# A gated mix of infini-attention and ReGLU on one core: the first chunk of x in four loads, four q products side by side, and a new written-out order of all engines

## The chip, the cores and the metric

The kernel runs on one core of a Trainium2 chip. The metric is the device time of one execution in microseconds (us); less is better. Five engines have queues of their own: TensorE (PE, whose weight loads are listed apart as PEld), VectorE (DVE), ScalarE (ACT), GpSimd (POOL) and SyncE (SP, which here only starts DMAs). Each engine runs its own list of instructions in order and waits on semaphores for the others.

## The reference

```python
# x: [1, 2048, 512] bf16; 32 heads of 16; 4 segments of 512 tokens; F = 1792
g = sigmoid((x * gate_w).sum(-1, keepdims=True))
# a: attention within a segment, and a memory M, z carried from segment to segment
for s in range(4):
    qs, ks, vs = q[:, :, s], k[:, :, s], v[:, :, s]          # q = x @ wq and so on
    p = softmax(qs @ ks.T * 0.25 + causal_mask)
    a_mem = (phi(qs) @ M) / (phi(qs) @ z + 1e-6)
    o_s = sigmoid(beta) * a_mem + (1 - sigmoid(beta)) * (p @ vs)
    M = M + phi(ks).T @ vs;  z = z + phi(ks).sum()           # phi(t) = t + 1 if t > 0 else exp(t)
a = concat(o_s) @ wo
# b: gated feed-forward
b = (relu(x @ W_gate) * (x @ W_up)) @ W_down
out = g * a + (1 - g) * b                                     # [1, 2048, 512] bf16
```

## The kernel before, in words

`program` (the body of `build_kernel`) writes down some 1,485 operations, each with the engine that may run it, what it reads and writes, and a cost. `Sched.run` then puts them on the engines in an order that is written out by hand: the table `ORDER` lists, for each engine, the numbers of the operations (a number counts the operations as `program` creates them). `Sched` derives the semaphore waits from what each operation reads and writes. Its costs, `LAND0`, `DCOST` and `landing`, are the planner's estimates of when a load lands; they served in the search for the order. `BANKS` gives one of eight PSUM banks to each product group (an `Epoch`). A product can start only when the engine that copies the bank's former content out of PSUM is done.

The work goes by segments of 512 tokens (a chunk of x). For each segment there are the q, k and v projections (`proj`, lines 574 and 576: products of 128x128 by 128x512, four over the features for each result), the attention (`att`), the memory products (`mu`, `nd`), the gate and up products with ReLU (`ffn`, line 800), and the output products (`outp`, lines 830 and 837). All are interleaved over segments by `ORDER`.

In `att` the scores of one segment are made in 18 *quads*. A quad (line 689) is up to 16 small products, four at a time in the four row groups of the array, that fill four PSUM banks with 2048 scores a partition. One ScalarE exponential (line 700) reads all four banks; GpSimd masks the diagonal parts (line 708); `pv` (line 738) multiplies the exponentials with v. There are 72 quads and 16 `pv`.

The start is special. The first chunk of x isn't transposed by a DMA. SyncE loads it as two halves of the tokens (`ldhT0`, `ldhT2`, 256 KB each) into the buffer hT, TensorE transposes it with an identity (line 511: eight operations `xt` of two products each, one for each half h and feature tile kt), and DVE or ACT copies the result into xT (line 518, `xc`). Until x comes, TensorE multiplies ones (line 502: five products of 512 columns and six of 128). The names of the loads: `ldwq0` to `ldwq3` are the four feature tiles of wq (128 KB each), likewise wk and wv; `ldwg0_k`, `ldwu0_k` the first half of the gate and up weights' columns (224 KB each), `ldwg1_k`, `ldwu1_k` the second half, which the operations `wg0_7` and later read; `ldx1_k` the transposing loads of the second chunk; `ldxr` plain loads of 128 rows of x, from which DVE computes the mixing gate (line 537, `gate0` to `gate15`, into the tile gl).

The kernel also warms ScalarE's exponential (`tab`, line 474) and starts three 1 KB loads from ScalarE (`ldtouch`, into adT).

Of the kernel before, what the change touches and what calls it, by code (L numbers as in the profile page):

```python
# [17 lines left out]
DCOST = {"ldwg0_0": 1000.0, "ldbraw": 1800.0, "ldgwb": 1300.0, "ldx1_0": 1500.0, "vsh0": 1100.0, "vsh1": 1100.0, "vsh2": 1100.0, "vsh3": 1100.0}  # L18
LAND0 = {"ldhT0": 2850.0, "ldhT2": 3100.0, "ldwq0": 3150.0, "ldwq1": 3200.0, "ldwq2": 3100.0, "ldwq3": 3000.0}
# [3 lines left out]
SPLIT = {2: (2,), 4: (4,), 5: (4, 1), 6: (4, 2)}  # L23
CORDER = [[(0, 1, 7, 2, 6, 3, 5, 4), (4, 0, 1, 7, 2, 6, 3, 5)] * 2] * 4
BANKS = ("130453107213460547754000000570000447000004700055766574475646577645465476647467556655640576747455500000450000656000104500"
         "045657464754775776575664507457667554544570454745665500000570000567000006700045657677645665465655776754467567546467670577"
         "54726660000067000067000004500045445454545645656647647546563023146")
ORDER = {k: [int(x) for x in v.split()] for k, v in {
    "pe": """
# [16 lines left out]
1459 1446 1440 1465 1460 1441 1447 1442 1466 1461 1448 1462 1449 1450 1467 1451 1468 1452 1469 1470 1471 1475 1472 1476 1477 1478 1479 1480 1481 1482""",  # L46
    "act": """
# [4 lines left out]
1272 129 1278 1052 1290 1296 1302 1189 1391 1308 1338 1314 1409 1326 1332 1415 1433 1453 1463""",  # L52
    "dve": """
# [9 lines left out]
1288 1421 1422 1322 1323 1345 1344 1346 1434 1324 1347 1348 1349 1350 1443 1473 1483""",  # L63
    "pool": """
# [8 lines left out]
1316 1335 1333 1334 1336 1330 1340""",  # L73
    "sp": """
0 1 2 3 7 6 8 9 4 11 15 5 21 17 13 10 12 16 14 26 18 85 37 23 19 83 156 20 22 36 38 24 182 81 25 181 199 200 39 30 27 157 29 45 87 28 42 31 40 43 92
44 94 93 96 98 100 41 468 469 470 347 346 544 107 471 109 543 105 371 111 370 527 492 113 106 532 120 542 694 502 537 888 118 122 512 887 693 718 119
717 124 522 876 126 871 846 886 836 881 1222 131 1205 1210 866 1221 856 132 1215 1220 1180 1170 1190 1444 1200 1454 1464 1474 1484""",
# [825 lines left out]
```

## Time and profile before

| | |
|---|---|
| median of 3 runs | 265.17 us (264.95 to 265.46) |
| profiled execution, its own time | 265.06 us |
| span of the profiled execution | 263.0 us |
| PE busy | 254.9 us (97%) |
| ACT, DVE, POOL busy | 185.6, 176.7, 121.3 us |
| DMA | 19.86 MB, mean 76 GB/s |

The span runs from the first to the last instruction of the profile; 2.06 us of the execution's own time lie outside it. "Idle before, releaser" in a row of the timeline is the time for which that engine had nothing running before the instruction, and what ended it.

### The profile page before, as it was taken

Reading aid. Unit: us, or ns where it says so; the run is one execution under the profiler, and the core shown is the slowest. Engines: PE = TensorE matmul, PEld = TensorE weight load, DVE = VectorE, ACT = ScalarE, POOL = GpSimd, SP = SyncE. Lnnn points to the kernel's source line nnn. Section 1 sums busy time; section 2 is a strip of 40 time slices with the busy share of each in tenths; the row PEclk is TensorE's granted clock in tenths of the full one; section 3 lists DMA queues with packets and bytes.
Section 4 is the critical chain, followed back from the end, with each engine's and each line's share of the span. In section 5 each row is a group of like instructions: output and inputs, shape, how many; then the busy total and the mean of one; then the engine's idle time right before and its main releaser. Section 6 shows DMA issues by size and latency. Waiting matters only on the chain.

```text
span 263.0 us, 6393 instructions
## 1 busy us (share of the span) xinstructions
PE 254.9 (97%) x2617; PEld 113.9 (43%) x2653; DVE 176.7 (67%) x350; ACT 185.6 (71%) x162; POOL 121.3 (46%) x295
## 2 busy tenths in 40 slices
PE   8999989999999999999999999999999999999996
PEld 4334433434444454444453544444444444444444
DVE  2587578878777477877788667677877533585821
ACT  4588777889888888887986667778676775674001
POOL 2024544665656455463846376636238342716000
PEclk9999999999999999999999999999999999999999
DMA  6998974009263221300036303000115101000002
GB/s 201 312 243 196 224 191 45 23 21 294 51 142 83 63 62 43 61 3 2 0 85 135 72 0 82 2 0 2 31 35 124 23 0 42 20 2 2 0 23 79
DMA packets 34924, 19.86 MB, mean 76 GB/s; under 512 B 24016, under 2 KB 34128, under 8 KB 34896
## 3 DMA queue, kind: packets, MB, share of 16 engines
q1 hardware_dynamic: 34800, 19.46, 30.3%
q8 instruction: 21, 0.34, 0.6%
q10 hardware_dynamic: 96, 0.00, 0.2%
q14 instruction: 7, 0.06, 0.1%
HBM read 10.40 MB, written 2.11 MB: 48 GB/s over the span
## 4 chain that ended last, share of the span: by engine, by line
PE 93%; DVE 2%; issue 2%; DMA 2%
PE ps L800 36%; PE ps L837 19%; PE ps L576 10%; PE ps L689 8%; PE ps L738 6%; PE ps L574 5%; PE ps L830 5%; DMA osb<-in_A_x_dram 2%; PE ps L632 1%; PE ps L502 1%; PE ps L511 1%; PE ps L615 0%; DVE osb L537 0%; DVE hT L811 0%; DVE Mc L620 0%
## 5 line engine op out<-in xcount | busy, mean ns | idle before, releaser
L700 ACT ACTIVATE E<-ps 128x2048 bf16<-128x2048 f32 x72 | 135.1, 1876 | 39.1 <-PE ps L689 38.7
L708 POOL TENSOR_SCALAR_AFFINE_SELECT E<-E 64x256 bf16<-64x256 bf16 (+1 forms) x256 | 101.2, 422 | 100.3 <-ACT E L700 89.5
L800 PE MATMUL ps<-xT,wu 128*128 128x512 bf16 x217 | 60.1, 380 | 1.5 <-issue 0.6
L800 PE MATMUL ps<-xT,wg 128*128 128x512 bf16 x214 | 58.2, 379 | 1.3 <-issue 1.0
L837 PE MATMUL ps<-wd,hT 128*128 128x512 bf16 (+2 forms) x227 | 56.4, 366 | 1.2 <-issue 1.0
L811 DVE TENSOR_TENSOR hT<-ps,rl 128x512 bf16<-128x512 f32 x56 | 38.2, 687 | 27.6 <-PE ps L800 25.8
L800 PEld LDWEIGHTS ps<-xT,wg 128*128 128x128 bf16 x224 | 20.8, 98 | 25.8 <-issue 1.9
L837 PEld LDWEIGHTS ps<-wd,hT 128*128 128x128 bf16 x238 | 21.3, 98 | 23.9 <-issue 3.0
L800 PEld LDWEIGHTS ps<-xT,wu 128*128 128x128 bf16 x224 | 19.6, 98 | 26.1 <-issue 4.7
L746 DVE STREAM_TRANSPOSE Tn<-ps 128x512 f32<-128x512 f32 x32 | 21.4, 699 | 10.6 <-PE ps L738 10.6
L689 PE MATMUL ps<-qT,kp 32*128 32x384 bf16 (+7 forms) x512 | 28.6, 287 | 0.0
L809 DVE TENSOR_SCALAR rl<-ps 128x512 bf16<-128x512 f32 x30 | 20.6, 688 | 8.0 <-PE ps L800 7.9
L808 ACT ACTIVATE rl<-ps 128x512 bf16<-128x512 f32 x26 | 15.5, 596 | 9.8 <-PE ps L800 9.8
L755 POOL TENSOR_TENSOR adT<-Tn,rdg 128x512 bf16<-128x512 f32 x12 | 12.9, 1074 | 14.7 <-DVE rdg L753 14.6
L689 PEld LDWEIGHTS ps<-qT,kp 32*128 32x128 bf16 x512 | 8.2, 92 | 24.9 <-issue 13.1
L845 DVE TENSOR_SCALAR osb<-ps,omg 128x512 bf16<-128x512 f32 (+2 forms) x13 | 9.2, 710 | 14.6 <-PE ps L830 8.8
L738 PE MATMUL ps<-E,vaug 64*17 64x128 bf16 (+7 forms) x512 | 18.7, 283 | 0.0
L738 PE MATMUL ps<-E,vsh 64*17 64x128 bf16 (+7 forms) x512 | 18.3, 283 | 0.0
L576 PE MATMUL ps<-xT,wk 128*128 128x512 bf16 x63 | 17.7, 380 | 0.1
L576 PE MATMUL ps<-xT,wq 128*128 128x512 bf16 x60 | 17.4, 380 | 0.4 <-issue 0.3
L574 PE MATMUL ps<-wv,xT 128*128 128x512 bf16 x62 | 16.7, 380 | 0.3 <-issue 0.2
L830 PE MATMUL ps<-wo,oT 128*128 128x512 bf16 (+2 forms) x67 | 16.4, 366 | 0.2 <-issue 0.2
(67 smaller groups left out, 216.1 us busy)
## 6 DMA issues: line engine op xcount, KB each, us to landing
vsh<-vaug SPq DMA_DIRECT2D x8, 272.0 KB, 3.6
osb<-in_A_x_dram SPq DMA_DIRECT2D x16, 128.0 KB, 2.6
out_dram<-osb SPq DMA_DIRECT2D x15, 128.0 KB, 2.0
wg<-in_B_W_gate_dram SPq DMA_DIRECT2D x8, 224.0 KB, 3.9
wu<-in_B_W_up_dram SPq DMA_DIRECT2D x8, 224.0 KB, 3.8
wd<-in_B_W_down_dram SPq DMA_DIRECT2D x1, 1792.0 KB, 7.8
hT<-in_A_x_dram SPq DMA_DIRECT2D x2, 256.0 KB, 3.0
wq<-in_A_wq_dram SPq DMA_DIRECT2D x4, 128.0 KB, 3.4
```

Of the source, the lines that this page charges most:

```text
L574: ins = e.matmul(A(ep)[:, :], lhsT=V.xT[:, kt, tok + col * 128:tok + (col + 1) * 128], rhs=w[:, kt, :], start=(kt == 0), stop=(kt == KT - 1))
L576: ins = e.matmul(A(ep)[:, :], lhsT=w[:, kt, col * 128:(col + 1) * 128], rhs=V.xT[:, kt, tok:tok + 512], start=(kt == 0), stop=(kt == KT - 1))
L689: ins = q.matmul(dst, lhsT=V.kp[r, kslot(s, G), c, :], rhs=V.qT[r, qslot(s, G), q0:q0 + w], start=True, stop=True, tile_position=(32 * jj, ...
L700: return a.activation(V.E[:, base * 512 + c0:base * 512 + c0 + n], PF[:, x.bank * 512:x.bank * 512 + n], ACT.Exp, scale=SCALE)
L708: pool(lambda g, ap=ap, lim=lim, pat=pat: g.affine_select(out=ap, in_=ap, compare_op=ALU.is_ge, fill=0.0, base=lim, pattern=[[0, 4]] + pat ...
L738: ins = q.matmul(A(eps[p])[32 * jj:32 * jj + 17, 64 * (c + u):64 * (c + u + n)], lhsT=v[:, 8 * G + 2 * jj + p, :], rhs=V.E[r, f:f + 64 * n ...
L746: dve(lambda e, p=p, ep=eps[p]: e.transpose(V.Tn[:, 2 * (G % (TNN // 2)) + p, :], A(ep)[:, :]), t_dve(512), writes=[f"Tn{2 * (G % (TNN // ...
L800: ins = e.matmul(A(ep)[:, :], lhsT=w[:, kt, f * 128:(f + 1) * 128], rhs=V.xT[:, kt, c % XR * 512:(c % XR + 1) * 512], start=(kt == 0), sto ...
L809: ("dve", lambda e, ep=eg, r=r: e.tensor_scalar(V.rl[:, r, :], A(ep)[:, :], 0.0, None, ALU.max), t_dve(512))],
L811: dve(lambda e, ep=eu, r=r, hs=hs: e.tensor_tensor(V.hT[:, hs, :], A(ep)[:, :], V.rl[:, r, :], ALU.mult), t_dve(512), reads=[f"rl{r}"], wr ...
L830: ins = e.matmul(A(ep)[:, 0:c1 - c0], lhsT=V.oT[:, ot[G], i * 128:(i + 1) * 128], rhs=V.wo[:, G, c0:c1], start=st_ and G == 0, stop=sp_ an ...
L837: ins = e.matmul(A(ep)[:, 0:c1 - c0], lhsT=V.hT[:, slots[f], i * 128:(i + 1) * 128], rhs=V.wd[:, f, c0:c1], start=st_ and f == f0, stop=sp ...
```

## The change

1. The first chunk of x is loaded in four pieces of 128 KB instead of two of 256 KB: half h of the tokens, half f of the features, in the order (h0, f0), (h1, f0), (h0, f1), (h1, f1). A row's run in memory is 512 bytes a token instead of 2 KB for two tokens.
2. The transposes run in that order too, and the copies are shared out anew: DVE has those of feature tiles 0 and 2, ACT those of 1 and 3. Three 128-column products of ones instead of six stand before them.
3. The q products of the first segment go feature tile by feature tile for all four results in four banks, and only then come the k products. Before, q and k were mixed.
4. The first wq tile is loaded by ScalarE, behind the warming exponential, which is now ScalarE's first instruction. The three 1 KB loads are gone.
5. The planner's landing times are changed (later landings between 5 and 45 us), and the order of all engines and the banks are searched anew. Every operation after the loads has a number lower by one. Ten of the operations that may run on either engine move from DVE to ACT.
6. `att` is rewritten so that a quad could be split over several visits; the table `SEVEN` that would do so is empty, so each of the 72 visits is one whole quad of the same products. The exponential's view of PSUM and E is now three-dimensional.

The loads in the code, with all else cut:

```diff
-LAND0 = {"ldhT0": 2850.0, "ldhT2": 3100.0, "ldwq0": 3150.0, "ldwq1": 3200.0, "ldwq2": 3100.0, "ldwq3": 3000.0}
+LAND0 = {"ldwq0": 2750.0, "ldwq1": 3200.0, "ldwq2": 3100.0, "ldwq3": 3000.0}
...
+SEVEN = [(), (), (), ()]
...
+    act(lambda e: e.activation(V.eb[:, 0:8], nc.const_aps.tensor(1.0, [128, 8], BF16), ACT.Exp), 1450, writes=["eb"], name="tab")
     x0 = A_x[0, 0:512, :].rearrange("(h p i) d -> h p i d", h=2, i=2)
     for h in range(2):
-        load("sp", [f"hT{2 * h}", f"hT{2 * h + 1}"], V.hT[:, 2 * h:2 * h + 2, :], x0[h], 1 << 18)
+        for f in range(2):
+            load("sp", [f"hx{h}_{f}"], V.hT[:, 2 * h:2 * h + 2, 256 * f:256 * f + 256], x0[h, :, :, 256 * f:256 * f + 256], 1 << 17)
     for eng, nm, w, src in (("sp", "wq", V.wq, A_wq), ("sp", "wk", V.wk, A_wk), ("sp", "wv", V.wv, A_wv)):
         for kt in range(KT):
-            load(eng, [f"{nm}{kt}"], w[:, kt, :], src[kt * 128:(kt + 1) * 128, :], 1 << 17)
+            load("act" if (nm, kt) == ("wq", 0) else eng, [f"{nm}{kt}"], w[:, kt, :], src[kt * 128:(kt + 1) * 128, :], 1 << 17)
...
-    act(lambda e: e.activation(V.eb[:, 0:8], nc.const_aps.tensor(1.0, [128, 8], BF16), ACT.Exp), 1450, writes=["eb"], name="tab")
-    for n, w in enumerate((W_g, W_u, W_d)):
-        load("act", [f"touch{n}"], V.adT[0:16, 32 * n:32 * n + 32], w[0:16, 0:32], 1024)
...
-    for m, n, role in ((5, 512, "w"), (6, 128, "w2")):
+    for m, n, role in ((5, 512, "w"), (3, 128, "w2")):
...
-    for h, kt, eng in ((0, 0, "dve"), (0, 1, "act"), (0, 2, "act"), (1, 0, "dve"), (0, 3, "dve"), (1, 1, "act"), (1, 2, "dve"), (1, 3, "act")):
+    for h, kt, eng in ((0, 0, "dve"), (0, 1, "act"), (0, 2, "dve"), (0, 3, "act"), (1, 0, "dve"), (1, 1, "act"), (1, 2, "dve"), (1, 3, "act")):
...
-                    return a.activation(V.E[:, base * 512 + c0:base * 512 + c0 + n], PF[:, x.bank * 512:x.bank * 512 + n], ACT.Exp, scale=SCALE)
+                    return a.activation(V.E[:, n * 512:(n + k) * 512].rearrange("q (b n) -> q b n", n=512)[:, :, 0:W], PS[:, x.bank:x.bank + k, 0:W], ACT.Exp, scale=SCALE)
```

The numbers of `ORDER` with their names put in, where the prediction speaks of them (a name stands once for each of its operations; `q0_2` is result 2 of q in segment 0, one product each time; `k0_2` and `v0_2` two products each time):

```
PE before: warm warm xt0 xt2 xt1 xt4 xt5 xt3 xt7 xt6 q0_3 q0_0 q0_3 q0_1 q0_0 k0_1 k0_0 k0_1 k0_0 k0_2 q0_2 q0_0 k0_2
           q0_0 q0_3 q0_1 q0_1 k0_3 q0_1 q0_3 k0_3 v0_0 quad ...
PE after:  warm warm xt0 xt1 xt4 xt5 xt2 xt3 xt6 xt7 q0_0 q0_1 q0_2 q0_3 (four times) k0_0 k0_3 k0_2 k0_1
           k0_0 k0_1 k0_3 k0_2 v0_2 v0_1 quad ...
PE before, later: pv0_0 mu0 quad wg0_7 q1_1 wg0_7 q1_0 q1_0 q1_1 quad wu0_7 ...
PE after, later:  pv0_0 mu0 quad k1_1 k1_0 k1_1 q1_1 k1_0 q1_1 quad q1_0 wg0_7 q1_0 wg0_7 wg0_8 wg0_8 wg0_10 quad wu0_7 ...
DVE before: ... hm0_6 tr0_0_1 tr0_0_0 gate3 reb mum0 qcp1_0 ...
DVE after:  ... hm0_5 tr0_0_0 reb tr0_0_1 gate3 gate1 kcp1_0 gate4 kmask0_2_1 mum0 ...
SP before: hT0 hT2 wq0 wq1 wk1 wk0 wk2 wk3 wq2 ...     ldxr3 is the 45th, ldwg1_1 the 35th, ldwu1_3 the 48th
SP after:  hx0_0 hx1_0 hx0_1 hx1_1 wq1 wq2 wq3 wk0 wk1 wk2 wk3 wv0 ...     ldxr3 is the 42nd, ldwg1_1 the 45th, ldwu1_3 the 50th
```

(`xt4` to `xt7` are those of the second half of the tokens; `mum0` on DVE empties the bank of `mu0`; `reb` is a reciprocal.)

More of the change, by code (lines that the diff above doesn't have):

```diff
@@ L670, in visit @@
             for G, c, u, n in parts:
-                for jj in range(4):
-                    f = jj * W + o
-                    while f < jj * W + o + 64 * n:
-                        g = min((f // 512 + 1) * 512, jj * W + o + 64 * n)
-                        steps.append((f - jj * W, jj, G, c, 64 * (c + u) + f - jj * W - o, f, g - f))
-                        f = g
+                steps.append((o, G, c, 64 * (c + u), 64 * n))
                 for v in range(n):
-                    at.setdefault((G, c), {})[u + v] = (base * 512, W, o + 64 * v, vid)
+                    at.setdefault((G, c), {})[u + v] = (base * 512, 512, o + 64 * v, vid)
                 if u == 0:
@@ L681, in visit @@
                 o += 64 * n
-            steps.sort(key=lambda x: (x[0], -x[1]))
-            def fq(q):
-                for _, jj, G, c, q0, f, w in steps:
-                    r = slice(32 * jj, 32 * jj + 32)
-                    i, j = part[f // 512]
-                    dst = PS[:, eps[i].bank + j, f % 512:f % 512 + w]
-                    ins = q.matmul(dst, lhsT=V.kp[r, kslot(s, G), c, :], rhs=V.qT[r, qslot(s, G), q0:q0 + w], start=True, stop=True, tile_position=(32 * jj, 0), skip_group_check=True)
-                return ins
@@ L703, in visit @@
-            runs = [[d] for d in diag]
-            for i, xs in enumerate(runs):
-                dims, pat = ([[xs[1] - xs[0], len(xs)]], [[0, len(xs)]]) if len(xs) > 1 else ([], [])
-                for h, lim in ((64, 0), (128, 64)):
-                    ap = bass.AP(V.E[:].tensor, base * 512 + xs[0], [[NBLK * 512, h], [W, 4]] + dims + [[1, 64]])
-                    pool(lambda g, ap=ap, lim=lim, pat=pat: g.affine_select(out=ap, in_=ap, compare_op=ALU.is_ge, fill=0.0, base=lim, pattern=[[0, 4]] + pat + [[1, 64]], channel_multiplier=-1),
-                                      t_pool(256 * len(xs)), reads=[f"E{base + j}" for j in range(nb)] + ([f"V{vid}m0_{i}"] if lim else []), writes=[f"V{vid}m{lim}_{i}"], name=f"mask{name}")
@@ L710, in visit, with fx @@
-            vres[vid] = [f"E{base + j}" for j in range(nb)] + [f"V{vid}m{lim}_{i}" for lim in (0, 64) for i in range(len(runs))]
+            return base, W, vid, steps, diag, sorted({p[0] for p in parts})
+        def visit(pieces):
+            eps, todo, rd = [], [], set()
+            for (base, W, vid, steps, diag, Gs), rows in pieces:
+                ep = Epoch("main", len(rows))
+                eps.append(ep)
+                for o, G, c, q0, w in steps:
+                    todo += [(o, -j, ep, i, G, c, q0, w) for i, j in enumerate(rows)]
+                rd |= {f"kp{kslot(s, G)}_{h}" for G in Gs for h in range(2)} | {f"qT{qslot(s, G)}" for G in Gs}
+            for x in eps:
+                x.group = eps
+            todo.sort(key=lambda x: x[:2])
+            def fq(q):
+                for o, j, ep, i, G, c, q0, w in todo:
+                    r = slice(-32 * j, 32 - 32 * j)
+                    ins = q.matmul(PS[:, ep.bank + i, o:o + w], lhsT=V.kp[r, kslot(s, G), c, :], rhs=V.qT[r, qslot(s, G), q0:q0 + w], start=True, stop=True, tile_position=(-32 * j, 0), skip_group_check=True)
+                return ins
+            W = max(x[0][1] for x in pieces)
+            name = f"{s}_{pieces[0][0][5][0]}_{vctr[0]}"
+            vctr[0] += 1
+            pe(fq, W / 2.4 + 10.0, reads=sorted(rd), writes=[x.res for x in eps[1:]], name=f"quad{name}", mode="r", ep=eps[0], role="w")
+            for ((base, W, vid, steps, diag, Gs), rows), x in zip(pieces, eps):
+                k, n = len(rows), base + rows[0]
+                def fx(a, x=x, W=W, k=k, n=n):
+                    return a.activation(V.E[:, n * 512:(n + k) * 512].rearrange("q (b n) -> q b n", n=512)[:, :, 0:W], PS[:, x.bank:x.bank + k, 0:W], ACT.Exp, scale=SCALE)
+                act(fx, t_act(k * W), writes=[f"E{n + i}" for i in range(k)], name=f"exp{name}", ep=x, role="r")
+                left[vid] = left.get(vid, 4) - k
+                if left[vid] == 0:
+                    for i, o in enumerate(diag):
+                        for h, lim in ((64, 0), (128, 64)):
+                            ap = bass.AP(V.E[:].tensor, base * 512 + o, [[NBLK * 512, h], [512, 4], [1, 64]])
+                            pool(lambda g, ap=ap, lim=lim: g.affine_select(out=ap, in_=ap, compare_op=ALU.is_ge, fill=0.0, base=lim, pattern=[[0, 4], [1, 64]], channel_multiplier=-1),
+                                 t_pool(256), reads=[f"E{base + j}" for j in range(4)] + ([f"V{vid}m0_{i}"] if lim else []), writes=[f"V{vid}m{lim}_{i}"], name=f"mask{s}_{Gs[0]}_{vid}")
+                    vres[vid] = [f"E{base + j}" for j in range(4)] + [f"V{vid}m{lim}_{i}" for lim in (0, 64) for i in range(len(diag))]
@@ L754, in flush @@
             av = V.adT[:, :].rearrange("q (c p e) -> q p c e", p=2, e=16)
-            (dve if s == NSEG - 1 else pool)(lambda e: e.tensor_tensor(av, Tv[:, :, :, 0:16], gv.unsqueeze(3).to_broadcast([128, 2, 16, 16]), ALU.mult), 690 if s == NSEG - 1 else 1100, reads=tn + [f"rdg{G % 2}"], writes=["adT"] + ([f"touch{n}" for n in range(3)] if s + G == 0 else []), name=f"ad{s}_{G}")
+            (dve if s == NSEG - 1 else pool)(lambda e: e.tensor_tensor(av, Tv[:, :, :, 0:16], gv.unsqueeze(3).to_broadcast([128, 2, 16, 16]), ALU.mult), 690 if s == NSEG - 1 else 1100, reads=tn + [f"rdg{G % 2}"], writes=["adT"], name=f"ad{s}_{G}")
             os_ = (s * 4 + G) % OTN
@@ L765, in att @@
         last = {G: max(i for i, t in enumerate(todo) if t[0] == G) for G in range(4)}
-        i0 = 0
-        for k, units in enumerate(UNITS[s]):
+        i0, quads, ends = 0, [], {}
+        for units in UNITS[s]:
             parts = []
@@ L773, in att, with get @@
                     parts.append([G, c, u, 1])
+            quads.append((parts, [G for G in range(4) if i0 <= last[G] < i0 + units]))
             i0 += units
-            visit(parts)
-            while carry and carry[0][3] < qctr[0] - 1:
+        made = {}
+        def get(k):
+            if k not in made:
+                made[k] = quad(quads[k][0])
+            return made[k]
+        k, visits = 0, []
+        while k < len(quads):
+            if k in SEVEN[s]:
+                visits += [[(k, A4)], [(k + 1, (0, 1, 2))], [(k + 2, A4)], [(k + 1, (3,)), (k + 3, (0, 1))], [(k + 4, A4)], [(k + 3, (2, 3)), (k + 5, (0,))], [(k + 6, A4)], [(k + 5, (1, 2, 3))]]
+                k += 7
+            else:
+                visits.append([(k, A4)])
+                k += 1
+        for n, v in enumerate(visits):
+            visit([(get(k), rows) for k, rows in v])
+            while carry and all(left.get(x) == 0 for x in carry[0][3]) and carry[0][4] < vctr[0] - 1:
                 flush()
-            if k == 0:
+            if n == 0:
                 between()
                 vsh_dma(s)
-            for G in range(4):
-                if i0 - units <= last[G] < i0:
-                    carry.append((s, G, at, qctr[0] - 1))
+            for k, rows in v:
+                for G in quads[k][1]:
+                    if left[made[k][2]] == 0:
+                        carry.append((s, G, at, [made[j][2] for j in range(len(quads)) if j in made and any(p[0] == G for p in quads[j][0])], vctr[0] - 1))
         if s == NSEG - 1:
```

63 lines of the change are left out of this document (25 added, 38 removed), and 74 rows, old and new, of the table ORDER.

## The prediction

> **What bounds the kernel now.** I read the page's busy times first, then PE's own list of waits, then busy time by stage, then the timeline of the two stages in which PE loses something.
>
> ```profile
> span 263.0 us, 6393 instructions
> PE 254.9 (97%) x2617; PEld 113.9 (43%) x2653; DVE 176.7 (67%) x350; ACT 185.6 (71%) x162; POOL 121.3 (46%) x295
> PEclk9999999999999999999999999999999999999999
> PE 93%; DVE 2%; issue 2%; DMA 2%
> ```
>
> PE is busy for 97% of the span at full granted clock, and the chain that ended last is PE for 93%. So only what PE waits for, or does too early or too late, can change the time. PE's list of waits, longest in total first (total, times, longest):
>
> ```profile
> PE ps L800 <- issue: 1.6, 10, 0.2
> PE ps L837 <- issue: 1.0, 6, 0.2
> PE ps L502 <- PEq L888: 0.8, 1, 0.8
> PE ps L800 <- DVE Mc L620: 0.5, 1, 0.5
> ```
>
> The "issue" waits are many of at most 0.2 us. They stand where PE goes between quads, `pv` and full products. Counted in the two order tables, there are 164 such changes before and 164 after, and no two quads are neighbours in either. So this cost stays. Only one wait on another engine is longer than 0.2 us. By stage (start:end, length, PE busy, PEld, DVE, ACT, POOL, clock, DMA share, GB/s):
>
> ```profile
> 5.30:12.30 7.00, 6.95 (x31) 2.67 (x31) 3.68 (x10) 3.74 (x9) 0.00 (x0) 1.00 0.97 304
> 36.40:37.00 0.60, 0.06 (x1) 0.07 (x2) 0.60 (x3) 0.55 (x1) 0.55 (x2) 1.00 0.48 158
> 37.00:255.00 218.00, 214.14 (x2277) 95.10 (x2309) 153.36 (x302) 159.06 (x134) 109.90 (x260) 1.00 0.21 49
> 255.00:263.00 8.00, 5.66 (x43) 3.34 (x41) 0.97 (x2) 1.27 (x2) 0.00 (x0) 1.00 0.24 78
> ```
>
> From 37 to 255 us PE idles 3.9 of 218 us, in the small steps above: nothing to win there, only to lose. The tail (2.3 us without PE) is the last piece's copy and store; both orders end with seven pairs of 128-column products and an output product, so I cost it at nothing. Two places are left: the head up to 12.3 us, and a hole of 0.54 us at 36.4.
>
> **The head, now.** Timeline (start, length, engine, what; idle before and who ended it):
>
> ```profile
> 0.80 1.28 ACT L518 ACT_TABLE_LOAD   x1 [0.80 <-PEq L888]
> 0.81 0.86 SPq L448 DMA_DIRECT2D hT<-in_A_x_dram  x2
> 0.84 2.93 PE L502 MATMUL ps<-const-bfloat16-1.0 128*128 128x512 bf16 x11 [0.84 <-PEq L888]
> 1.65 0.15 PEld L502 LDWEIGHTS ps<-const-bfloat16-1.0 128*128 128x128 bf16 x1 [0.28 <-issue]
> 1.72 0.90 SPq L448 DMA_DIRECT2D wq<-in_A_wq_dram  x2
> 2.08 0.15 PEld L502 LDWEIGHTS ps<-const-bfloat16-1.0 128*128 128x128 bf16 x1 [0.28 <-issue]
> 3.67 1.67 PE L511 MATMUL ps<-ident,hT 128*128 128x128 bf16 x16
> 4.10 0.42 DVE L518 CAST xT<-ps 128x256 bf16<-128x256 f32 x1 [4.10 <-PE ps L511]
> 4.39 0.77 PEld L511 LDWEIGHTS ps<-ident,hT 128*128 128x128 bf16 x10 [0.17 <-DMA hT<-in_A_x_dram]
> 4.53 1.45 ACT L518 ACTIVATE xT<-ps 128x256 bf16<-128x256 f32 x4 [2.44 <-PE ps L511]
> 5.31 1.25 PE L576 MATMUL ps<-xT,wq 128*128 128x512 bf16 x5
> 5.85 0.22 ACT L474 ACTIVATE eb<-const-bfloat16-1.0 128x8 f32<-128x8 bf16 x1
> 6.53 0.55 PEld L576 LDWEIGHTS ps<-xT,wk 128*128 128x128 bf16 x4 [0.47 <-DMA wk<-in_A_wk_dram]
> 7.53 0.98 PEld L576 LDWEIGHTS ps<-xT,wk 128*128 128x128 bf16 x6 [0.45 <-DMA wk<-in_A_wk_dram]
> 12.39 0.10 PEld L689 LDWEIGHTS ps<-qT,kp 32*128 32x128 bf16 x4 [0.42 <-ACT qT L582]
> ```
>
> The first q product starts at 5.31. The order puts 31 full products between there and the first quad, which starts about 0.1 us after the last of them (12.39), so they end at 12.29. The pace of such products is that of this piece of the chain (start, length, what), 0.216 us each:
>
> ```profile
> 52.03 2.16 PE ps L574 x10
> ```
>
> 31 x 0.216 = 6.70 us, but 12.29 - 5.31 = 6.98: 0.28 us are lost in the head, where the weight loads wait for wk.
>
> **The head, after.** Let S be the start of the first q product; the 31st product then ends at S + 6.70 if no load is late. S is the latest of three things.
>
> (a) *x and its transposes.* The two 256 KB loads let PE go at 3.67 and 4.39, 0.72 us apart, so 128 KB are worth 0.36: the first quarter is there at 3.67 - 0.36 = 3.31. SP starts a load each 0.45 us (0.81 to 1.72 for two), so the others come at 3.76, 4.21, 4.66. Four products each at 0.10 (1.67 us for 16) fit into 0.45, so PE ends the transposes at about 5.1. The first tile of features needs only the quarters of 3.31 and 3.76. DVE's copy starts 0.43 after its product (3.67 to 4.10) and takes 0.42; the second is done at 3.76 + 0.85 = 4.61. The first q result also takes over the bank of a transpose that ACT copies (0.36, a quarter of 1.45): two products later, 4.78.
>
> (b) *wq0.* The table load ends at 2.08, the warming exponential takes 0.22, so ScalarE starts the load at 2.30. This start hides before ACT's first copy (3.9 at the earliest). Landing: the wq loads took (minimum, median, maximum), and a 1 KB load from ScalarE took 2.4:
>
> ```profile
> DMA to landing us min/median/max: 3.0/3.4/3.7
> adT<-in_B_W_gate_dram ACTq DMA_DIRECT2D x1, 1.0 KB, 2.4
> ```
>
> So between 4.7 and 5.7 (2.4 and 3.4); I take 3.0, the value of the first wq load, which also went out while x was on its way: 5.30. It is (b) that decides: S = 5.3, no earlier than before.
>
> (c) *the rest.* Feature tile 1 is needed at S + 0.86 = 6.2; wq1 is now SP's fifth load, out at 2.6, landing at 3.4 later at 6.0. The next tiles have 0.86 each against 0.47 between loads. The k products start at S + 3.45 = 8.8, when wk0 and wk1 (eighth and ninth, out at 4.1 and 4.5) are there since about 8. In the new order the loads that PE waited for come before their use.
>
> So the 31st product ends at 5.3 + 6.70 = 12.0 against 12.29: **-0.3 us**. Ends: S = 5.1 gives -0.5, S = 5.7 gives +0.1. The three ones-products less remove nothing: they'd end at 0.84 + 5 x 0.43 + 3 x 0.10 = 3.3, when x lands. (0.43 is the step from the row at 1.65 to that at 2.08.)
>
> **The hole at 36.4.**
>
> ```profile
> 31.09 0.52 SPq L536 DMA_DIRECT2D osb<-in_A_x_dram  x1
> 32.48 1.31 DVE L746 STREAM_TRANSPOSE Tn<-ps 128x512 f32<-128x512 f32 x2 [0.33 <-PE ps L738]
> 33.53 0.38 PE L800 MATMUL ps<-xT,wg 128*128 128x512 bf16 x1 [0.16 <-issue]
> 35.38 0.93 DVE L537 CUSTOM_DVE_ANT_0 osb<-osb,gwb 128x512 bf16<-128x512 bf16 x1 [1.59 <-DMA osb<-in_A_x_dram]
> 36.51 0.37 DVE L620 TENSOR_TENSOR Mc<-Mc,ps 128x272 f32<-128x272 f32 x1
> 36.94 0.60 PE L800 MATMUL ps<-xT,wu 128*128 128x512 bf16 x2 [0.54 <-DVE Mc L620]
> ```
>
> SP started ldxr3 only at 31.09; it landed 4.3 us later. DVE stood 1.59 us before `gate3`, `mum0` came late, and PE waited 0.54 us for `mu0`'s bank. After, ldxr3 is SP's 42nd load instead of the 45th, some three starts (about 3 us at this stage) earlier, so it lands near 32.4, before DVE is through its transposes (33.8 now). And `mu0`'s bank is next used by `wg0_10`, 14 products later than `wu0_7` was. What is late next on DVE: `gate1` and `gate4` stand before `mum0` too, 0.93 each, which that distance (3 us) covers. So **-0.54 us**; ends -0.6 and 0 (if ldxr1 or ldxr4 are late instead).
>
> **The rest of the order.** The same products, quads and `pv`. Ten copies move from DVE to ACT, 0.6 us each by the profile's groups (mean in ns, then idle before):
>
> ```profile
> L700 ACT ACTIVATE E<-ps 128x2048 bf16<-128x2048 f32 x72 | 135.1, 1876 | 39.1 <-PE ps L689 38.7
> L809 DVE TENSOR_SCALAR rl<-ps 128x512 bf16<-128x512 f32 x30 | 20.6, 688 | 8.0 <-PE ps L800 7.9
> L808 ACT ACTIVATE rl<-ps 128x512 bf16<-128x512 f32 x26 | 15.5, 596 | 9.8 <-PE ps L800 9.8
> ```
>
> ACT goes from 185.6 to 191.6 us of 263: cover enough on average, but quads stand as close as 2.6 us in both orders and an exponential takes 1.88, so a single ACT copy in such a gap just fits. The shortest way from a bank's last product to its next use is 1.1 to 1.3 us in both orders (counted in products), against 0.69 for a DVE copy. The present order has this tightness and shows no wait over 0.2 us after 37 us. I take +0.1 us for the new one; ends 0 and +1.2 (two holes like that at 36.4). The three touch loads were off PE's path: 0. The rewritten `att` emits the same quads, and its exponential reads the same 2048 contiguous values: 0.
>
> **Sum.** Against the profiled execution's 265.06 us (0.11 under the median of 265.17): 265.06 - 0.3 - 0.54 + 0.1 = **264.3 us**. About 0.2% (0.53 us) is what a measurement of this kernel can tell from no change; 264.3 is 0.3% under the median.
>
> **Rivals.**
>
> *The head gives nothing and the new order has its own small holes.* For: S hangs on a load whose price I have only from other queues, and tightness is the same. With S at 5.7 (+0.1) and half a microsecond of new waits: 265.06 + 0.1 - 0.54 + 0.5 = 265.1, no change. Chance 0.22.
>
> *Slower: the second half of the feed-forward weights comes after its need.* ldwg1_1 moves from SP's 35th place to its 45th. The 45th start was at 31.09 with as many transposing loads ahead (nine of 44 in both), so it lands near 35.4 at the 4.3 us of that load. `wg0_7` needs it; it ran at 33.53 and now has 14 more products ahead: 33.5 - 0.3 + 3.0 = 36.2. Cover 0.8 us. Each microsecond that it lands after 36.2 is one lost, since all that follows on PE stands behind it. At 6.6 us from start to landing the total is above 265.7. Against: the longest of the transposes here, which queue with it, took 5.2:
>
> ```profile
> DMA to landing us min/median/max: 3.0/3.1/5.2
> ```
>
> Then 265.8 or more. Chance 0.10.
>
> *Slower: the array comes up to full pace later.* In the trace products of 512 columns step by 0.43 us at 1.65 and by 0.216 later; full pace came between 4.4 and 5.3, about 4 us after the first product at 0.84, although the granted clock reads 1.00 throughout. If pauses between the x quarters make this count start anew, say at 3.3, full pace comes at 7.3 and the products from 5.3 to 7.3 lose half: +1.0. If it starts anew at 4.66 it comes at 8.7: +1.7, and 264.3 + 1.7 = 266.0. Against: the ones end at 3.3 when x comes, and four products fill 0.40 of each 0.45 us. [...] Chance 0.08.
>
> **How the numbers follow.** The forecast (263.9 to 264.6) has 0.54, a better one (S near 5.1, no new wait) 0.06, no change 0.22, the two slower ones 0.18. Faster 0.60, same 0.22, slower 0.18. The range of 8 in 10 goes from 263.7, a little under the sum of the good ends (265.06 - 0.5 - 0.6 = 264.0), to 265.8, where the slower cases begin.
>
> **What would show it.** In the changed profile: transposes from 3.3, first q product at 5.1 to 5.5, 16 q products without a wait for wq or wk, first quad 36 products after the first q product, near 13.1; no PE wait for Mc near 36 us, and DVE not standing before line 537; PE's list of waits with nothing over 0.2 us besides the start; PE's work the same. I'm wrong if PE shows a wait for wq after 5.7, for wg or wu between 33 and 42 us, products stepping by 0.43 after 5.3, or new waits for DVE or ACT that sum to over half a microsecond.

## The result: 0.4% slower, and the profile after

| | before | after |
|---|---|---|
| median | 265.2 us (264.6 to 265.73, 16 runs) | 266.3 us (265.25 to 268.33, 16 runs) |
| ratio after / before | | 1.0042 [1.0028, 1.0057] |
| profiled execution, its own time | 265.06 us | 266.75 us |
| its span | 263.0 us | 264.7 us |

The change made the kernel 1.1 us slower in the median; 0.7 us faster was forecast. The page of after:

```profile
span 264.7 us, 6420 instructions
PE 260.3 (98%) x2650; PEld 114.3 (43%) x2650; DVE 171.6 (65%) x340; ACT 191.0 (72%) x172; POOL 122.7 (46%) x295
PEclk9999999999999999999999999999999999999999
PE 97%; DMA 1%; SPq 1%; DVE 0%; issue 0%
```

PE is the bound as before, and the granted clock is full. That PE is "busy" 5.4 us longer is not more work; more on this in the point-by-point section. The chain is PE for 97%; what DVE and "issue" had in it before, 2% each, is gone. PE's list of waits is short (total, times, longest):

```profile
PE ps L512 <- DMA hT<-in_A_x_dram: 1.2, 3, 0.7
PE ps L503 <- PEq L904: 0.8, 1, 0.8
```

The wait for Mc at 36.4 us is gone, and nothing after the head waits at all. The stages that answer to those of before (columns as there) say the same:

```profile
5.30:12.30 7.00, 6.59 (x29) 3.10 (x30) 1.61 (x4) 1.97 (x5) 0.00 (x0) 1.00 0.91 264
36.40:37.00 0.60, 0.60 (x4) 0.29 (x3) 0.60 (x3) 0.60 (x1) 0.00 (x0) 1.00 0.73 266
37.00:255.00 218.00, 218.00 (x2314) 94.75 (x2312) 148.02 (x293) 165.99 (x146) 112.22 (x264) 1.00 0.24 53
```

So the loss stands in the head. Its timeline (start, length, engine, what; idle before and who ended it):

```profile
0.81 2.65 SPq L450 DMA_DIRECT2D hT<-in_A_x_dram  x4
0.84 2.61 PE L503 MATMUL ps<-const-bfloat16-1.0 128*128 128x512 bf16 x8 [0.84 <-PEq L904]
2.34 0.40 ACTq L450 DMA_DIRECT2D wq<-in_A_wq_dram  x1
3.69 1.04 PE L512 MATMUL ps<-ident,hT 128*128 128x128 bf16 x8 [0.23 <-DMA hT<-in_A_x_dram]
5.47 0.61 PE L512 MATMUL ps<-ident,hT 128*128 128x128 bf16 x4 [0.75 <-DMA hT<-in_A_x_dram]
6.32 0.61 PE L512 MATMUL ps<-ident,hT 128*128 128x128 bf16 x4 [0.24 <-DMA hT<-in_A_x_dram]
6.72 3.47 PE L577 MATMUL ps<-xT,wq 128*128 128x512 bf16 x10
7.15 0.15 PEld L577 LDWEIGHTS ps<-xT,wq 128*128 128x128 bf16 x1 [0.28 <-issue]
...
8.86 0.15 PEld L577 LDWEIGHTS ps<-xT,wq 128*128 128x128 bf16 x1 [0.28 <-issue]
9.17 0.75 PEld L577 LDWEIGHTS ps<-xT,wq 128*128 128x128 bf16 x4 [0.17 <-issue]
```

Two things are to be read here. *x is late*: SP needs 2.65 us for the four starts, the third and fourth quarter let PE go at 5.47 and 6.32, and the first q product starts at 6.72 instead of 5.31, +1.41. *The array is slow*: the weight loads of the q products stand 0.43 apart (five rows from 7.15 to 8.86) until 9.17; before, the products after 5.31 were at full pace already. From 6.72 to 9.17 half of the time is lost, (9.17 - 6.72) / 2 = 1.2 us. The span is 1.7 us longer: 1.41 + 1.2 - 1.7 leaves 0.9 us that the rest of the new order wins back.

### The profile page after: what moved, and what is told of

Its sections match the earlier page's. It is cut to its first block, busy times and chain, and to the rows that moved or that the text cites. A ratio compares the mean times of both kernels' runs of the same rounds, so it can differ in the third digit from the quotient of the medians.

```text
span 264.7 us, 6420 instructions
## 1 busy us (share of the span) xinstructions
PE 260.3 (98%) x2650; PEld 114.3 (43%) x2650; DVE 171.6 (65%) x340; ACT 191.0 (72%) x172; POOL 122.7 (46%) x295
## 4 chain that ended last, share of the span: by engine, by line
PE 97%; DMA 1%; SPq 1%; DVE 0%; issue 0%
PE ps L816 38%; PE ps L853 19%; PE ps L577 11%; PE ps L690 9%; PE ps L737 7%; PE ps L846 5%; PE ps L575 5%; DMA hT<-in_A_x_dram 1%; PE ps L633 1%; PE ps L616 1%; SPq L450 1%; PE ps L512 0%; DVE osb L861 0%
## 5 line engine op out<-in xcount | busy, mean ns | idle before, releaser
L816 PE MATMUL ps<-xT,wu 128*128 128x512 bf16 x224 | 61.5, 380 | 0.0
L816 PE MATMUL ps<-xT,wg 128*128 128x512 bf16 x224 | 60.5, 380 | 0.0
L853 PE MATMUL ps<-wd,hT 128*128 128x512 bf16 (+2 forms) x238 | 57.7, 367 | 0.0
L825 DVE TENSOR_SCALAR rl<-ps 128x512 bf16<-128x512 f32 x29 | 19.8, 686 | 10.4 <-PE ps L816 10.3
L577 PE MATMUL ps<-xT,wq 128*128 128x512 bf16 x64 | 18.5, 402 | 0.0
L577 PE MATMUL ps<-xT,wk 128*128 128x512 bf16 x64 | 16.3, 380 | 0.0
L737 PEld LDWEIGHTS ps<-E,vaug 64*17 64x17 bf16 x512 | 11.6, 86 | 8.5 <-issue 4.9
```

Source lines behind the costliest of these rows:

```text
L577: ins = e.matmul(A(ep)[:, :], lhsT=w[:, kt, col * 128:(col + 1) * 128], rhs=V.xT[:, kt, tok:tok + 512], start=(kt == 0), stop=(kt == KT - 1))
L737: ins = q.matmul(A(eps[p])[32 * jj:32 * jj + 17, 64 * (c + u):64 * (c + u + n)], lhsT=v[:, 8 * G + 2 * jj + p, :], rhs=V.E[r, f:f + 64 * n ...
L816: ins = e.matmul(A(ep)[:, :], lhsT=w[:, kt, f * 128:(f + 1) * 128], rhs=V.xT[:, kt, c % XR * 512:(c % XR + 1) * 512], start=(kt == 0), sto ...
L825: ("dve", lambda e, ep=eg, r=r: e.tensor_scalar(V.rl[:, r, :], A(ep)[:, :], 0.0, None, ALU.max), t_dve(512))],
L853: ins = e.matmul(A(ep)[:, 0:c1 - c0], lhsT=V.hT[:, slots[f], i * 128:(i + 1) * 128], rhs=V.wd[:, f, c0:c1], start=st_ and f == f0, stop=sp ...
```

## The experiments

All are kernels with small edits; where operations fall away, the order tables are renumbered. "Time" is the median of 5 to 16 runs (but for the one marked) with the lowest and highest; the kernel before had 265.20 to 265.24 beside them. "Full pace" is the moment, read from the profiled execution, at which the products' step halves (0.43 to 0.216 us for 512 columns, 0.107 to 0.055 for 128); "x there" and "wq0 there" are the landings of the x loads and of the first wq tile; "q" is the first q product.

| kernel | time, us | ratio to before | x there | wq0 there | q | full pace |
|---|---|---|---|---|---|---|
| before | 265.2 | | 3.62, 4.35 | 4.74 | 5.3 | 4.9 |
| after | 266.3 (265.25–268.33) | 1.0042 [1.0028, 1.0057] | 3.64, 4.05, 5.42, 6.27 | 4.61 | 6.7 | 9.2 |
| after, run once more | 265.95, one run | | 3.53, 4.38, 5.41, 6.75 | 4.76 | 7.0 | 4.6 |
| old head in the new order | 264.49 (264.21–265.64) | 0.9973 [0.9958, 0.9989] | 3.38, 4.01 | 5.40 | 5.5 | 4.5 |
| two x loads, wq0 from ACT | 265.21 (264.7–267.2) | 1.0003 [0.9984, 1.0022] | 3.56, 4.19 | 6.20 | 6.2 | by 6.2 |
| four x loads, wq0 from SP | 266.72 (265.53–267.25) | 1.0039 [1.0022, 1.0056] | 3.47, 4.21, 4.94, 5.35 | 6.17 | 6.2 | 4.5 |
| x in four runs of 1 KB | 266.71 (264.9–267.32) | 1.0049 [1.003, 1.0069] | 2.89, 3.48, 3.87, 5.53 | 5.74 | 6.8 | 8.4 |
| wq0 from ACT, ahead of all | 266.66 (266.45–267.02) | 1.0057 [1.0039, 1.0076] | 4.09, 4.79 | 4.29 | 6.1 | 9.4 |
| pauses filled | 265.66 (265.38–266.07) | 1.001 [0.9998, 1.0021] | 3.57, 4.53, 5.24, 6.69 | 4.90 | 7.2 | 6.7 |
| pauses filled, wq0 from SP | 265.85 (265.27–266.33) | 1.0023 [1.001, 1.0036] | 3.56, 4.26, 5.33, 5.76 | 6.27 | 6.4 | 5.2 |
| old head, filled | 264.78 (264.18–265.34) | 0.9984 [0.9973, 0.9994] | 3.58, 4.23 | 4.55 | 6.1 | 6.3 |
| before, fewer ones | 265.64 (265.12–266.77) | 1.0022 [1.0008, 1.0036] | second 4.21 | 5.35 | 5.5 | 8.0 |
| before, ldxr3 earlier | 265.01 (264.69–265.56) | 0.9996 [0.9985, 1.0008] | 3.65, 4.33 | 5.03 | 5.2 | 4.0 |
| before, ldxr3 and ldwq3 earlier | 265.2 (264.79–265.45) | 0.9996 [0.9987, 1.0004] | 3.54, 4.31 | 5.25 | 5.4 | 6.7 |

### Is it the head? The old head in the new order

Two x loads of 256 KB as before, and wq0 as SP's third load; the order and banks of after otherwise.

```diff
         for f in range(2):
-            load("sp", [f"hx{h}_{f}"], ..., 1 << 17)
+        load("sp", [f"hx{h}_0", f"hx{h}_1"], V.hT[:, 2 * h:2 * h + 2, :], x0[h], 1 << 18)
-            load("act" if (nm, kt) == ("wq", 0) else eng, ...)
+            load(eng, ...)
```

> The changed kernel with x in two loads of 256 KB and wq0 from SyncE right behind them, as before; the order of the q products and of everything later as changed. Expected by the trace of the changed kernel (no wait of TensorE after its head): x at 3.65 and 4.35, first q product at 5.4 at full pace, no wait after: 264.4, faster than before by 0.3%. Rival (the new order is no better than the old): 265.2.

Measured 264.49 us, 0.9973 [0.9958, 0.9989]. It beats both kernels. The head's loads cost after 266.3 - 264.49 = 1.8 us, and all else in the change is worth -0.7 us. In its timeline the 16 q products run in one piece at full pace:

```profile
3.42 1.63 PE L514 MATMUL ps<-ident,hT 128*128 128x128 bf16 x16
5.54 3.61 PE L579 MATMUL ps<-xT,wq 128*128 128x512 bf16 x16 [0.48 <-DMA wq<-in_A_wq_dram]
```

### Which part of the head? Two x loads alone, and wq0 from SP alone

The first of these has only the upper half of the diff above (wq0 stays on ACT), the second only the lower half (x stays in quarters), with wq0 (operation 5) moved between the queues:

```diff
+ORDER["act"].remove(5)
+ORDER["sp"].insert(4, 5)
```

> The changed kernel with x in two loads of 256 KB as before, wq0 still from ScalarE, all else as changed. If the rows of 512 bytes made x late: x lands at 3.65 and 4.4, transposes end near 5.3, first q product at 5.4 at full pace, and the rest of the new order keeps its 0.9 us: 264.4. If the competition of wq0 made x late: the second half lands near 5.4, first q product near 6.2, part of it at half pace: 265.5 or above. If the new order loses time elsewhere: 265.2 or above although the head is like before.

> The changed kernel with the first wq tile loaded by SyncE as its fifth load, behind the four quarters of x. Theory (competition): wq0 from ScalarE, out at 2.34 and landed at 4.61 before two x quarters that went out at 2.20 and 2.84, pushed those back by about a microsecond; without it they land near 4.6 and 5.3 us, and the first q product waits for wq0 itself (out at 3.5, landed about 6.5): 266.2 or a little less. Rival (rows of 512 bytes): the x quarters land at 5.4 and 6.3 as now, first q product at 6.7 or later, 266.3 to 266.6.

With two x loads and wq0 from ACT, 265.21 us: the split of x costs 266.3 - 265.21 = 1.1. x was there at 3.56 and 4.19, but wq0 was late, which none of the expectations had. So the load from ACT isn't good either: it is worth 265.21 - 264.49 = +0.7 against SP. There, PE's wait and the load's row (from start to landing) read:

```profile
6.24 3.63 PE L577 MATMUL ps<-xT,wq 128*128 128x512 bf16 x16 [0.54 <-DMA wq<-in_A_wq_dram]
L451 ACTq DMA_DIRECT2D wq<-in_A_wq_dram x1: 385/385/385, 2.3 to 2.3; - x1
DMA to landing us min/median/max: 3.9/3.9/3.9
```

3.9 us for 128 KB that took 2.3 in after: here three wq loads of SP were out from 1.73 on and went in beside it.

With the quarters and wq0 from SP the competition shows from the other side. The x quarters (a start takes 0.59 to 0.70 us in both kernels), first in after, then here:

```profile
L450 SPq DMA_DIRECT2D hT<-in_A_x_dram x4: 586/608/697, 0.8 to 2.8; - x4
DMA to landing us min/median/max: 2.5/3.0/3.4
```

```profile
L452 SPq DMA_DIRECT2D hT<-in_A_x_dram x4: 586/608/692, 0.8 to 2.8; - x4
DMA to landing us min/median/max: 2.5/2.7/2.7
36.95 0.61 PE L579 MATMUL ps<-xT,wq 128*128 128x512 bf16 x2
38.51 0.59 PE L818 MATMUL ps<-xT,wg 128*128 128x512 bf16 x2 [0.95 <-DMA wg<-in_B_W_gate_dram]
```

Without the load from ACT the last quarter lands at 5.35 instead of 6.27: 0.9 us of x's lateness came from ACT's load. (Over all executions in the table: 5.35 and 5.76 without it, 6.27, 6.69 and 6.75 with it.) In after's trace, from 3.5 to 5.5 us, the packets of SP's queue took 63.6% of the time of the 16 DMA engines and those of ACT's queue 22.9%. In the execution profiled, q starts half a microsecond sooner than in after, at 6.2 and at full pace; it now waits for wq0, SP's fifth load, which lands at 6.17. But the time is no better (266.72), and the profile shows another loss: the second half of the gate weights came 0.95 us after its need, at 38.5 (last two rows). That is the prediction's second rival; in after itself there is no such wait. The place on SP explains little of it: the load went out at 32.88 instead of 32.61, but took 5.5 us to land instead of 4.2. In a kernel further down with the same order on SP ("pauses filled, wq0 from SP") it took 4.1, and nothing waited. In how many of the other runs it came late no profile shows, so how much of the 266.72 belongs to the head stays open.

### Shorter starts, and wq0 first

In the first kernel a quarter is 128 rows of 1 KB (one token of each pair) instead of 256 pieces of 512 bytes; each transpose then reads two of them, and SP starts both quarters of the first half before those of the second. In the second x is in two loads, and ACT's first instruction starts wq0, ahead of the exponential (3 and 0 are their numbers there), which it then no longer waits for.

```diff
-            load("sp", [f"hx{h}_{f}"], V.hT[:, 2 * h:2 * h + 2, 256 * f:256 * f + 256], x0[h, :, :, 256 * f:256 * f + 256], 1 << 17)
+            load("sp", [f"hx{h}_{f}"], V.hT[:, 2 * h + f, :], x0[h, :, f, :], 1 << 17)
```

```diff
+ORDER["act"][:2] = [3, 0]
```

> The changed kernel with the four 128 KB loads of x cut the other way: each takes one of the two tokens of a pair with all 512 features, so a row is 1 KB instead of 512 bytes and a load has 128 rows instead of 256. A transpose then needs both loads of its half. wq0 still from ScalarE. If the 512-byte rows make the starts (0.60 to 0.70 us each) and the landings long: a start takes 0.40 to 0.45 as other 128 KB loads, x is complete near 5.0 instead of 6.3, time near 265.3. If it is the competition with wq0: starts short, but the last x load still lands after 5.5 us, time 265.5 to 266.

> As the kernel with two loads of x and wq0 from ScalarE, but ScalarE starts wq0 as its very first instruction, ahead of the warming exponential, near 0.8 us. If only the late start (2.3 us) made ScalarE's wq0 late, it lands near 4.0, x half a microsecond later than with SyncE alone, first q product near 5.2: 264.3, like the old head or a little better. If a load on ScalarE's queue competes with x at any time: the second x half lands at 4.8 or later, q at 5.7: 264.6 or above.

Neither helps (266.71 and 266.66 us). The rows of the first, and one of the second:

```profile
L451 SPq DMA_DIRECT2D hT<-in_A_x_dram x4: 389/416/432, 0.8 to 2.2; - x4
DMA to landing us min/median/max: 2.1/2.2/3.3
5.57 1.46 PE L513 MATMUL ps<-ident,hT 128*128 128x128 bf16 x12 [1.44 <-DMA hT<-in_A_x_dram]
4.14 2.15 PE L513 MATMUL ps<-ident,hT 128*128 128x128 bf16 x16 [0.69 <-DMA hT<-in_A_x_dram]
```

The starts are short now (0.42 instead of 0.61), and three quarters land 2.1 to 2.2 us after their start, against 2.8 for the first quarter in after. The fourth, started at 2.2 beside ACT's load of 2.33, takes 3.3 and holds PE for 1.44 us. With wq0 ahead of all, both x loads come 0.45 us later than before and PE stands 0.69 us before the first. Both executions come to full pace late, at 8.4 and 9.4. With wq0 ahead of all q starts no later than with two x loads and wq0 behind the exponential (6.1 against 6.2), and still the time is 1.4 us more: in the profiles that is the pace.

### Is the pace lost through pauses? Filling them, and making one

"Pauses filled" is after with six small ones-products instead of three, and ten and seven more of 128 columns behind the second and third quarter's transposes, so that PE doesn't idle while x is late. "Before, fewer ones" takes products away ahead of x, so that PE idles before it comes.

```diff
-    for m, n, role in ((5, 512, "w"), (3, 128, "w2")):
+    for m, n, role in ((5, 512, "w"), (6, 128, "w2")):
+ORDER["pe"].insert(ORDER["pe"].index(68) + 1, 1484)     # ten ones behind xt5
+ORDER["pe"].insert(ORDER["pe"].index(64) + 1, 1485)     # seven behind xt3
```

```diff
-    for m, n, role in ((5, 512, "w"), (6, 128, "w2")):
+    for m, n, role in ((2, 512, "w"), (1, 128, "w2")):
```

> The changed kernel with TensorE kept at work while it waits for x: six 128-column products of ones at the start instead of three, ten more between the transposes of the second and the third quarter of x, seven more between the third and the fourth. No data of the result is touched. Theory (pace): the pause before the third quarter keeps the array at half pace; without it full pace comes near 4.9 us, the 16 q products step by 0.216 from the first (6.7 us) on, and the time falls by 1.1 us to about 265.2, with less spread between runs. Rival (the late pace has nothing to do with the pause): products still step by 0.43 until about 9 us, 266.3.

> The kernel before with a pause made by hand: two products of ones of 512 columns and one of 128 instead of five and six, so TensorE stands from about 1.8 us to the landing of x near 3.6. All else as before. Pace theory (a pause in the first microseconds makes the array come up to full pace later): products step by 0.43 until some 7 to 8.5 us in most runs, time +0.7 to +1.7 over before (265.9 to 266.9), with a wider spread. Rival (full pace comes a fixed time after the start whatever TensorE does): as before, 265.2.

Filled: 265.66 us, 0.6 under after, although q starts at 7.2, later than in after. The runs lie within 265.38 to 266.07. The 16 runs of after fall in two halves, eight from 265.25 to 266.07 and eight from 266.53 to 268.33; filling took away the upper half. (Late gate weights could lengthen a run too: in after's two profiles they landed 2.2 and 0.3 us before their need. Which of the upper runs are pace and which are that isn't shown.) In the filled kernel's profile the q products run at full pace from the first:

```profile
7.11 2.96 PEld L579 LDWEIGHTS ps<-xT,wq 128*128 128x128 bf16 x15
```

Fewer ones: 265.64 us, 0.4 slower than before, with the pause and the half pace as expected of a pace that pauses delay:

```profile
PE ps L511 <- DMA hT<-in_A_x_dram: 1.5, 1, 1.5
6.72 0.15 PEld L576 LDWEIGHTS ps<-xT,wq 128*128 128x128 bf16 x1 [0.27 <-issue]
7.14 0.15 PEld L576 LDWEIGHTS ps<-xT,wk 128*128 128x128 bf16 x1 [0.28 <-issue]
7.96 1.61 PEld L576 LDWEIGHTS ps<-xT,wk 128*128 128x128 bf16 x8 [0.23 <-issue]
```

That is less than the 0.7 to 1.7 expected, although half pace up to 7.96 costs (7.96 - 5.48) / 2 = 1.24 us. PE came to all that follows later, and its waits for wk (0.28) and for Mc (0.54) were gone: an old loss absorbed part of the new one.

Then two combinations, and after itself once more. The first adds the two order lines for wq0 from SP to the fills. The second adds six small ones to the old head, and these fills:

```diff
+ORDER["pe"].insert(ORDER["pe"].index(58) + 1, 1482)     # two ones behind xt1
+ORDER["pe"].insert(ORDER["pe"].index(70) + 1, 1483)     # five behind xt7
```

> The changed kernel with both edits tried alone before: wq0 from SyncE behind the four quarters of x, and products of ones in TensorE's pauses (six, ten and seven of 128 columns). If the loss is made of a late first q product and a late full pace: x lands near 4.9 and 5.4, first q product at 6.2 to 6.5 at full pace, 0.7 to 0.9 us later than with the old head, 265.2 to 265.4, with little spread. Rival (the parts don't add up because half rows cost something later too): 265.7 or above.

> The kernel with the old head and the new order, and TensorE kept at work in its pauses: six products of ones of 128 columns at the start instead of three, two more before the second half of x, five more while it waits for wq0. If a part of its runs still comes up to full pace late: the upper half of its times falls, median 264.3 to 264.5, no run above 265.2. If its pauses are too short to matter: as the old head alone, 264.5 with runs up to 265.6.

> The changed kernel itself, for a second profile. If its spread is that of the moment of full pace: the time follows that moment, about 0.5 us for each microsecond that it lies between the first q product and 9.1 us, and the order behind the head is again without a wait.

Filled with wq0 from SP takes 265.85 us: no less than filled with wq0 from ACT (265.66), and more than the 265.2 to 265.4 expected. It is 0.9 under the same loads without fills (266.72), but between the two profiles that is the wait for the gate weights and not the pace, since both come to full pace before q. The old head isn't helped either (264.78 against 264.49): there is no pause worth filling, and where the array is still slow the fills only delay q (6.1 instead of 5.5). After, run once more, is the telling one:

```profile
3.58 0.61 PE L512 MATMUL ps<-ident,hT 128*128 128x128 bf16 x4
4.43 0.43 PE L512 MATMUL ps<-ident,hT 128*128 128x128 bf16 x4 [0.25 <-DMA hT<-in_A_x_dram]
5.46 0.40 PE L512 MATMUL ps<-ident,hT 128*128 128x128 bf16 x4 [0.60 <-DMA hT<-in_A_x_dram]
6.80 0.40 PE L512 MATMUL ps<-ident,hT 128*128 128x128 bf16 x4 [0.94 <-DMA hT<-in_A_x_dram]
6.98 2.96 PEld L577 LDWEIGHTS ps<-xT,wq 128*128 128x128 bf16 x15
```

The same kernel, with x even later (q at 7.04), takes 265.95 instead of 266.75 us, because the array was at full pace before the long pauses (four transposes in 0.43 us from 4.43 on, 0.61 before) and kept it through pauses of 0.60 and 0.94. So the moment of full pace differs between executions of one kernel. From the first q product to PE's last end after needs 255.7 us and this execution 254.5, which is also what the old head, the two x loads with wq0 from ACT and all three filled kernels need (254.5 to 254.6). The late pace costs 1.2 us here, and the later q takes 0.3 of it back.

### The hole at 36.4 us by itself

Before, with SP starting ldxr3 as its 42nd load; then with ldwq3 as its tenth load too.

```diff
+ORDER["sp"].remove(87)
+ORDER["sp"].insert(41, 87)     # ldxr3
+ORDER["sp"].remove(5)
+ORDER["sp"].insert(9, 5)       # ldwq3, in the second kernel only
```

> The kernel before with one entry of SyncE's order moved: ldxr3, the load that gate3 waits for, is its 42nd start instead of its 45th. If the hole of 0.54 us at 36.4 us hangs on that load alone: DVE no longer stands before line 537, TensorE doesn't wait for Mc, 264.7. If another load or step is late in its place: 265.2.

> The kernel before with two entries of SyncE's order moved: ldxr3 as its 42nd start instead of its 45th, and the last wq tile as its 10th start instead of its 12th. If what the new order gains after its head is no more than that no load is late, mending the two late loads of the old order gives most of it: no wait for Mc near 36 us, none for wq near 9.5 us, 264.6. If the new order gains elsewhere (the 0.14 us waits for wk, the balance of ACT and DVE): 265.0 or above.

The hole goes, as costed: DVE goes through `gate3` at 34.07 without a wait (35.38 with 1.59 before). But PE waits for ldwq3 in the head instead:

```profile
34.07 0.65 DVE L539 CUSTOM_DVE_ANT_0 osb<-osb,gwb 128x512 bf16<-128x512 bf16 x1
PE ps L578 <- DMA wq<-in_A_wq_dram: 0.5, 1, 0.5
```

265.01 us, no difference that can be told. With both loads earlier the profiled execution has neither wait (its list holds only the start and 0.2 for wv), and the time is again that of before, 265.2. That execution came to full pace at 6.7 instead of 4.9, which costs its q and k products (6.66 - 5.40) / 2 = 0.63. Whether that holds for its other runs no profile shows, so why mending both waits gained nothing in the median stays open.

## Why the prediction was wrong, point by point

*That PE bounds, and only its waits and its pace count*: right. *The "issue" waits, 3.9 of 218 us*: wrong reading, without harm. The page of before has 2617 matmuls against 2653 weight loads, 36 fewer, and its trace has 36 idle steps of up to 0.2 us in PE besides the start and the wait for Mc; after has 2650 of each and, behind the head, no idle step. The kernel with ldxr3 and ldwq3 earlier has before's products and full records:

```profile
PE 259.8 (99%) x2653; PEld 114.6 (44%) x2653; DVE 177.1 (67%) x350; ACT 185.5 (70%) x162; POOL 120.7 (46%) x295
37.00:255.00 218.00, 218.00 (x2315) 95.14 (x2308) 153.54 (x302) 159.51 (x134) 109.97 (x262) 1.00 0.22 50
```

So these steps were absent records, not idle time, and PE's busy time can't be compared between two pages before the counts are.

*The head, S = 5.3*: wrong, measured 6.72. The step that failed is (a), the x quarters. Predicted to let PE go at 3.31, 3.76, 4.21 and 4.66; they landed at 3.64, 4.05, 5.42 and 6.27. Three errors are in it. First, half the bytes in pieces of 512 bytes were not there sooner: 128 KB took 2.8 us (0.81 to 3.64), and so did 256 KB before (0.81 to 3.62); I had taken 0.36 off for the missing half. It was the pieces, not the halving: with rows of 1 KB the first three quarters landed at 2.89, 3.48 and 3.87, ahead of the times in (a). Second, a start costs by its pieces too: 0.59 to 0.70 us for 256 pieces of 512 bytes, where I had 0.45 from loads of 128 rows; the four starts take 2.65 instead of 1.8, which puts the last one 0.7 later. Third, ACT's load of wq0 was in flight beside them and took 22.9% of the DMA engines' time from 3.5 to 5.5 us: 0.9 of the last quarter's lateness, by the kernel without it (0.5 to 1.4 over all executions above). I had priced wq0's landing beside x, and never x's landing beside wq0. Step (b), wq0 at 5.3, decided nothing: it landed at 4.61 while q waited for the last transposes, which PE's order puts ahead of it.

*The third rival, full pace late (0.08, 266.0 us)*: this is what happened in the profiled execution, with its 1.2 us. The argument against it, that four products fill 0.40 of each 0.45 us, fell with step (a). In the 14 profiles, with no pause over 0.6 us before it, full pace came between 4.0 and 6.7 (ten profiles; the earliest is 3.2 us behind the first product at 0.84), with one of 0.69 to 1.5 us between 8.0 and 9.4 (four profiles). After run once more is one of the ten: the array was at full pace by 4.6 there, and the long pauses came behind that. The rival's count of 4 us that starts anew was an estimate from the one trace of before, and no record shows what sets the moment of full pace. So that a pause delays it is the likeliest reading, not shown; that filling the pauses shortens the time (0.6 us) and making one lengthens it (0.4 us) is shown.

*The hole at 36.4, -0.54*: the hole went in after, in the old head's kernel and in both kernels with ldxr3 earlier. *The rest of the order, +0.1*: PE's list in after shows no wait behind the head, so nothing came of it. From the first q product to PE's last end it takes 254.5 us with the old head in the new order and 255.4 in before, 0.9 less; the hole (0.54) and the waits for wk (0.28) are most of that. q starts 0.2 later there (5.54 against 5.31), which leaves the 0.7 of the medians. But the medians of the two kernels on the old order didn't show the 0.54 by itself, so its share in the 0.7 isn't settled.

*The second rival, weights late*: not in after's two profiles (`wg0_7` waits for nothing), but it came in that of the kernel with wq0 from SP. The cover, costed at 0.8 us, was 2.2 in after, 0.3 in after run once more and 0.4 with the old head. In the profiles of after and of the two kernels with wq0 from SP behind the quarters the load took 4.2, 5.5 and 4.1 us from start to landing where I had 4.3, and this spread is wider than the cover costed.

In sum: the head, forecast at -0.3, cost 1.8 us against the old head in the same order, of which some 0.6 went with the pauses filled (pace, by the likeliest reading) and the rest is x's lateness. The -0.3 was the waits for wk, and these went with the new order, whatever the head. So the whole forecast of -0.74 is nearly what the old head in the new order gave (-0.7), in part by luck: q started 0.2 later than forecast there, and the new waits didn't come.

## What to carry to other kernels

Price each load of a first stage as a start on its queue (by its pieces: a median of 0.42 us for 128 rows of x here, 0.61 for 256 pieces), a landing, and what it takes from the other loads in flight, also from those on other queues (with ACT's load of wq0 the last quarter of x landed 0.9 us later than without it, and that load itself took 3.9 us beside three loads of SP, 2.3 in after); splitting a load that PE needs whole anyway, because its order puts all transposes first, added starts and gained nothing here. In the first microseconds an idle PE cost a wait here and, by the likeliest reading, a later full pace: filling the pauses of after took off 0.6 us, making one in the kernel before added 0.4. So cover it with products until the data is there, but not past that (in the old head the fills put q at 6.1 instead of 5.5). Where a head decides, profile a kernel more than once: the moment of full pace differed by over 4 us between two executions of the same kernel (9.2 and 4.6).

## What the runs showed of the hardware

- The granted clock reads 1.00 (0.999 once) in all these profiles, also where products step by 0.43 us up to 9.2 us. Half pace is seen in the step of weight loads, not in that column.
- A start on SP in the first 6 us took 0.39 to 0.48 us for 128 rows of 1 or 2 KB and 0.59 to 0.71 for 256 pieces of 512 bytes. The one load of 128 rows right behind such pieces took 0.60, in all five kernels that have them.
- The first 128 KB of x landed 2.1 us after the start as 128 rows of 1 KB (one profile) and 2.7 to 2.8 us after it as 256 pieces of 512 bytes (five profiles).
- The same 128 KB load from ACT, started at 2.33 to 2.34, took 2.3 to 2.6 us to land beside x in quarters of 512-byte pieces (three profiles), 3.4 beside quarters of 1 KB rows, and 3.9 beside three wq loads of SP.
